# One row of a folded DFT on other engines, earlier folds, and first weight blocks split in idle buffers

## The chip, the cores and the metric

The kernel runs on one core of one Trainium2 chip. Its engines are TensorE (PE in the profile; its weight loads are PEld), VectorE (DVE), ScalarE (ACT), GpSimd (POOL) and SyncE (SP), which issues most of the DMAs. Each engine works through its own queue in order and waits on semaphores for the others. The metric is the time of one execution on the device in microseconds; the median of the runs counts.

## What is computed

Attention masked by clusters of keys and queries, then a block that adds the real part of a two-dimensional Fourier transform, normalizes and runs an MLP, then a second MLP whose gate goes through a convolution over three tokens. Cut to what matters:

```python
def _attn_ref(q, k, v, centroids):            # 2 batches, 8 heads, 768 tokens, 64 wide
    mask = q_assign[:, :, :, None] == k_assign[:, :, None, :]   # nearest of 16 centroids
    scores = np.where(mask, scale * np.matmul(q, k.transpose(0, 1, 3, 2)), -1e9)
    attn = np.exp(scores - np.max(scores, axis=-1, keepdims=True))
    attn = attn / (np.sum(attn, axis=-1, keepdims=True) + 1e-09)
    return np.matmul(attn, v)

def _moe_ref(x, w_ch1, w_ch2):                # 512 -> 2048 -> 512
    u = x + np.real(np.fft.fft(np.fft.fft(x, axis=1), axis=2))
    un = (u - mean(u)) / np.sqrt(var(u) + 1e-06)
    return u + np.maximum(un @ w_ch1, 0.0) @ w_ch2

def _moe2_ref(x, w_in, conv_w, w_out):        # 512 -> 1024 -> 512
    h = np.maximum(x @ w_in, 0.0)
    gate = 1.0 / (1.0 + np.exp(-conv3(h, conv_w)))
    return h * gate @ w_out
```

The weights come as 64-bit words and are turned into float32 on the chip.

## The kernel before

**Precision.** Most products run in three passes (`pass3`, L84): each operand is a high part plus a low part (the value minus its high part), and high x high, high x low and low x high are summed. A "low part" is thus one elementwise subtraction, and a "high part" one cast.

**Attention** is a loop over 96 steps n (L791), six for each of the 16 heads, in an order written out by hand: within it each engine's queue holds the instructions as the code emits them. Step n computes the scores of step n + 8 with their row maxima (`score_max`, the maximum on VectorE, L571), the transposed scores and their exponentials for step n (`score_exp`: t products L601 and L603, exp on ScalarE L609), the high part of step n - 1's probabilities (`prob_hi`, L621, on ScalarE; on VectorE after step 87) and their low part (`prob_lo`, L629: on VectorE for the steps in `LO_ON_DVE`, on GpSimd for the others), and the product with V of step n - 3 (`attn_v`, L641). The scores, the t products and everything that borrows a bank take turns in three PSUM slots, so a t product needs the slot whose maximum was taken shortly before. Other work is hung into the steps with `at(list, step, function)`; within a step the lists come in the order pre, mid (inside `score_max`), aft, post, fill. So for each following pair of heads: loads, `prep_sims`, `prep_first` (L450, GpSimd), `prep_pick` (L454 and L456, VectorE), high and low parts of queries and keys (`prep_hi`, `prep_lo`: L490 to L499), `prep_turn`. At the end of each head `attn_out` divides and writes to U (L649 to L654); head 7, the last one of the first batch, is written at step 52. `max_turn` (L575 to L580) turns each head's maxima into a row that SP copies to where the t products read it.

**Mixing** (`mixing`, L95) is the Fourier transform of one batch by its symmetries. It folds U into even and odd halves (`fold`, L113 to L118), makes the one row that the fold leaves over ("row", L135 to L137), adds the halves ("even", L142), splits them (L122, L126), multiplies by cosines and sines (y, z, ab) and adds the result to U (`ab_add` L227, `ab_mirror` L235, on GpSimd). The first batch's stages hang in steps 54 to 76 (`plan`, L702); both of its folds run on GpSimd. The second batch's run beside the first MLP, as a generator (`later`, L991) that advances one stage or a few at each `next(side)`.

**Norm** (`norm`, L246) takes a batch's tiles of 128 tokens one at a time: statistics (L255 to L259, VectorE), a power on GpSimd (L264), scaling (L269), four transposes (L274), a copy on ScalarE and a low part on VectorE (L286). The first batch's six tiles start at steps 73, 76, 79, 82, 85 and 88.

**First MLP.** Per batch g and block f of 128 hidden columns: `mlp1_up` (24 matmuls, relu on ScalarE L872, low part on VectorE L874), then `down` (18 matmuls into six accumulators; after the tokens' tiles in `when` it advances the side work). The loop (L1019) does the up product of block f + 1 ahead of the down product of block f. In the first batch each weight block is loaded by SP into one of two `raw64` buffers, converted (`from64`: L299, L300, L302 and L304 on VectorE, L301 on ScalarE), squared for its norm (`squares`, L323, ScalarE) and split (`split_w`: wh by ScalarE L851, wl by VectorE L853). Blocks 0 and 1 are converted ahead during attention; block 0 is split into four mixing buffers from step 92 on (`first_split`). Blocks 9 to 15 have buffers only once the second batch's mixing has given back its pool (L997 to L1000). What lies outside the hand-written loop is placed into the queues by a planner of the compiler, which may issue an instruction earlier than the code has it.

**Second MLP**: as the first, with the convolution between. The change does not touch it.

## Time and profile before

| | us |
|---|---|
| runs shown (3) | 700.31, 701.77, 703.11; median 701.77 |
| profiled execution | 702.69 |
| its span, first to last instruction | 700.9 |
| around the span | 1.79 |
| TensorE busy | 667.3 |
| TensorE idle in the span | 33.6 |
| VectorE, ScalarE, GpSimd busy | 543.9, 410.8, 200.3 |
| attention's steps 0 to 95, start of the first t product to start of the last | 26.6 to 275.4 |
| first MLP's first up product starts | 280.3 |

The profile is one execution. An engine's busy time counts its own instructions only. In a timeline each line gives the start, the length, the engine, the line of the code, the operation, what is written and read, the shape and the count; in brackets stands how long the engine was idle before it and what ended that. Matmuls overlap in the array, so their lengths add up to more than the time they take; their starts tell the pace.

### The profile page before, as it was taken

Reading aid. Unit: us, or ns where it says so; the run is one execution under the profiler, and the core shown is the slowest. Engines: PE = TensorE matmul, PEld = TensorE weight load, DVE = VectorE, ACT = ScalarE, POOL = GpSimd, SP = SyncE. Lnnn points to the kernel's source line nnn. Section 1 sums busy time; section 2 is a strip of 40 time slices with the busy share of each in tenths; the row PEclk is TensorE's granted clock in tenths of the full one; section 3 lists DMA queues with packets and bytes.
Section 4 is the critical chain, followed back from the end, with each engine's and each line's share of the span. In section 5 each row is a group of like instructions: output and inputs, shape, how many; then the busy total and the mean of one; then the engine's idle time right before and its main releaser. Section 6 shows DMA issues by size and latency. Waiting matters only on the chain.

```text
span 700.9 us, 12789 instructions
## 1 busy us (share of the span) xinstructions
PE 667.3 (95%) x5106; PEld 504.6 (72%) x5106; DVE 543.9 (78%) x873; ACT 410.8 (59%) x664; POOL 200.3 (29%) x168
## 2 busy tenths in 40 slices
PE   8799999998899997989999999999999999999997
PEld 6598988987799886869998998555555555555553
DVE  7777889898877997999469976997634399867662
ACT  3478869787458787536335654676534367555442
POOL 8156658568646945121041000000000000000000
PEclk9999999999899999999999999999999999999999
DMA  7747696773633413224203350243000000001002
GB/s 219 198 110 193 158 244 157 213 209 84 155 87 78 106 62 122 68 98 144 113 0 121 121 180 10 77 156 122 0 2 1 1 0 1 1 1 71 20 1 90
DMA packets 22087, 66.50 MB, mean 95 GB/s; under 512 B 4502, under 2 KB 7562, under 8 KB 19212
## 3 DMA queue, kind: packets, MB, share of 16 engines
q1 hardware_dynamic: 21020, 61.94, 31.0%
q0 software_dynamic: 1008, 3.75, 2.0%
q8 instruction: 40, 0.66, 0.4%
q14 instruction: 19, 0.16, 0.1%
HBM read 40.94 MB, written 5.77 MB: 67 GB/s over the span
## 4 chain that ended last, share of the span: by engine, by line
PE 72%; DVE 16%; DMA 4%; issue 2%; ACT 2%; POOL 2%; SPq 1%; DVEq 0%; ACTq 0%; POOLq 0%
PE acc L86 8%; PE acc L87 8%; PE acc L85 8%; PE up L85 5%; PE up L87 5%; PE up L86 5%; PE av L641 5%; PE s L566 3%; PE t L601 3%; PE s L568 3%; PE t L603 3%; DVE m L571 3%; PE sim L440 3%; PE u L85 2%; PE u L87 2%
## 5 line engine op out<-in xcount | busy, mean ns | idle before, releaser
L629 POOL TENSOR_TENSOR p<-p,p 128x768 f16<-128x768 f32 x62 | 107.5, 1735 | 85.7 <-ACT p L621 59.5
L571 DVE TENSOR_REDUCE m<-s 128x1 f32<-128x768 f32 x96 | 90.5, 947 | 13.8 <-PE s L568 6.5
L609 ACT ACTIVATE p<-t,cbias 128x768 f32<-128x768 f32 x92 | 82.8, 900 | 26.2 <-PE t L603 25.0
L621 ACT CAST p<-p 128x768 f16<-128x768 f32 x88 | 73.0, 830 | 1.2
L641 PE MATMUL av<-V,p 128*128 128x65 f16 x1728 | 70.8, 195 | 2.8 <-POOL p L629 2.8
L641 PEld LDWEIGHTS <-p 128*128 128x128 f16 x1728 | 59.3, 99 | 18.3 <-issue 15.1
L601 PE MATMUL t<-X 128*128 128x384 f32 x192 | 54.5, 365 | 8.6 <-DVE m L571 6.9
L566 PE MATMUL s<-X 128*128 128x384 f32 x192 | 56.2, 374 | 3.2 <-DMA X<-ohd 1.8
L568 PE MATMUL s<-Y 96*128 96x384 f32 x192 | 50.0, 341 | 1.1 <-DMA Y<-G 1.1
L603 PE MATMUL t<-Y 98*128 98x384 f32 x192 | 50.2, 343 | 0.0
L85 PE MATMUL up<-un,wha 128*128 128x384 f32 x120 | 41.3, 344 | 2.7 <-DVE YcL L163 1.3
L85 PE MATMUL u<-x,wb 128*128 128x384 f16 x128 | 41.7, 326 | 1.3 <-DVE h L892 0.9
L87 PE MATMUL up<-un,wla 128*128 128x384 f32 x120 | 40.5, 338 | 1.8 <-DVE wla L853 1.8
L601 PEld LDWEIGHTS t<-X 128*128 128x128 f32 x192 | 32.0, 192 | 13.9 <-issue 6.7
L85 PE MATMUL up<-un,wa 128*128 128x384 f16 x128 | 41.7, 326 | 0.0
L87 PE MATMUL up<-un,wa 128*128 128x384 f16 x128 | 41.7, 326 | 0.0
L86 PE MATMUL up<-un,wa 128*128 128x384 f16 x128 | 41.7, 326 | 0.0
L87 PE MATMUL u<-x,wb 128*128 128x384 f16 x128 | 41.7, 326 | 0.0
L86 PE MATMUL u<-x,wb 128*128 128x384 f16 x128 | 41.7, 326 | 0.0
L86 PE MATMUL up<-un,wha 128*128 128x384 f32 x120 | 40.5, 338 | 0.0
L629 DVE TENSOR_TENSOR p<-p,p 128x768 f16<-128x768 f32 x30 | 37.7, 1257 | 0.1
L85 PE MATMUL acc<-wb,gH 128*128 128x512 f16 x96 | 36.4, 379 | 0.5 <-ACT gH L900 0.5
(368 smaller groups left out, 1701.0 us busy)
## 6 DMA issues: line engine op xcount, KB each, us to landing
rawa<-w SPq DMA_DIRECT2D x14, 1024.0 KB
rawb<-w SPq DMA_DIRECT2D x8, 1024.0 KB
raw<-qk SPq DMA_DIRECT2D x7, 768.0 KB
X<-G SPq DMA_DIRECT2D x14, 384.0 KB
Y<-G SPq DMA_DIRECT2D x14, 384.0 KB
vraw<-v SPq DMA_DIRECT2D x8, 384.0 KB
out<-y SPq DMA_DIRECT2D x12, 256.0 KB
X<-G SPq DMA_DIRECT2D x14, 192.0 KB
```

Of the source, the lines that this page charges most:

```text
L85: T.matmul(o, sH, mH, start=start, stop=False)
L86: T.matmul(o, sH, mL, start=False, stop=False)
L87: T.matmul(o, sL, mH, start=False, stop=stop)
L566: T.matmul(t[:, c, 0:384], X[:, 0, sl], X[:, 1, 384 * c:384 * c + 384], start=True, stop=False)
L568: T.matmul(t[:, c, 0:384], Y[0:96, 0, sl], Y[0:96, 1, 384 * c:384 * c + 384], start=False, stop=True)
L571: V.tensor_reduce(m6s[h][:, i:i + 1], t[:, :, 0:384], AX.XY, ALU.max, negate=True)
L601: T.matmul(t[:, c, 0:384], X[:, 1, sl], X[:, 0, 384 * c:384 * c + 384], start=True, stop=False)
L603: T.matmul(t[:, c, 0:384], Y[0:98, 1, sl], Y[0:98, 0, 384 * c:384 * c + 384], start=False, stop=True)
L609: A.activation(p, t[:, :, 0:384], AF.Exp, bias=cbias, scale=0.125)
L621: A.copy(p16[:, 0], p32s[n])
L629: eng.tensor_sub(p16[:, 1], p, p16[:, 0])
L641: T.matmul(o, p16[:, k, 128 * j:128 * j + 128], v16[:, i, h % 2, 65 * part:65 * part + 65], start=(i + j + k + part == 0), stop=(i == 5), ...
```

## The change

- The mixing's "row" is cut into four stages: a subtraction on GpSimd (step 54), a copy on ScalarE (56), a subtraction on GpSimd (56), a copy on ScalarE (58). Before, it was three instructions on VectorE at step 57. The second batch's row changes with it.
- The first batch's even folds start at steps 52 and 53 instead of 54 and 55.
- Low parts of steps 55, 71, 79, 83 and 85 go from VectorE to GpSimd, that of step 94 from GpSimd to VectorE. The two low parts of the last pair of heads (`prep_lo`, step 69) go from GpSimd to VectorE.
- Norm's six tiles start at steps 72, 75, 78, 80, 83 and 85.
- The bfloat16 identity is made at step 84 on GpSimd; before, it was made outside the loop on VectorE.
- The first up product of the MLP stands in the attention loop, at steps 96 and 97, in attention's PSUM slots; block 0 is split at steps 91 to 94; block 1 is split into the mixing's buffers YcH and YcL at steps 96 and 97.
- The squares of blocks 0 and 1 move to rounds 11 and 12 of the first MLP. Round f (1 to 13) asks for block f + 2; before, round f (0 to 12) asked for block f + 3. The conversions are issued one block after another. Round 0 advances the side work once, not twice.

```diff
 LO_ON_DVE = ({n for n in range(54) if n % 12 in (2, 7, 8, 10)}
-             | {n for n in range(54, 87) if n % 12 in (1, 2, 7, 11)} | {87})
+             | {59, 61, 62, 67, 73, 74, 86, 87, 94})
...
-            r1 = dp.tile([1, N2], F32, tag="row", bufs=1, name=f"r1{b}")
-            ev = d["ev", 0], d["ev", 1]
-            V.tensor_sub(r1[:, 0:257], ev[0][0:1, 0, 0:257], ev[1][0:1, 0, 0:257])
-            V.tensor_copy(Zx[0:1, 0:257], r1[:, 0:257])
-            V.tensor_sub(Zx[32:33, 0:257], r1[:, 0:257], f32(Zx[0:1, 0:257]))
+            r1 = d["r1"] = dp.tile([1, N2], F32, tag="row", bufs=1, name=f"r1{b}")
+            G.tensor_sub(r1[:, 0:257], d["ev", 0][0:1, 0, 0:257], d["ev", 1][0:1, 0, 0:257])
+
+        @stage("rowH")
+        def _():
+            A.copy(Zx[0:1, 0:257], d["r1"][:, 0:257])
+
+        @stage("rowL")
+        def _():
+            G.tensor_sub(d["r1"][:, 0:257], d["r1"][:, 0:257], f32(Zx[0:1, 0:257]))
+
+        @stage("rowZ")
+        def _():
+            A.copy(Zx[32:33, 0:257], d["r1"][:, 0:257])
...
+    A_LOADS = [()] + [(f + 2,) for f in range(1, 14)] + [()] * 2
...
-        for op in from64(w, raw):
-            op()
+        with tc.issue_after(last_op[0]) if last_op else nullcontext():
+            for op in from64(w, raw):
+                i = op()
+            last_op[:] = [i.ins]
...
-                at(fill, k + 9, prep_lo, m, 0, G)
+                at(fill, k + 9, prep_lo, m, 0, G if m < 7 else V)
...
-                at(fill, k + (10 if m < 7 else 9), prep_lo, m, 1, G)
+                at(fill, k + (10 if m < 7 else 9), prep_lo, m, 1, G if m < 7 else V)
...
-        plan = (("even0", fill, 54), ("even1", fill, 55), ("row", aft, 57), ("even", fill, 58), ("evenH", aft, 59),
-                ("evenL", fill, 59),
+        plan = (("even0", fill, 52), ("even1", fill, 53), ("row", fill, 54), ("rowH", aft, 56), ("rowL", fill, 56),
+                ("even", fill, 58), ("rowZ", fill, 58), ("evenH", aft, 59), ("evenL", fill, 59),
...
-        for i, t in enumerate((0, 3, 1, 4, 2, 5)):
-            n = 73 + 3 * i
+        for n, t in zip((72, 75, 78, 80, 83, 85), (0, 3, 1, 4, 2, 5)):
...
-        at(fill, 92, first_split, 0)
-        at(fill, 93, first_split, 1)
-        at(fill, 95, first_split, 2)
-        at(fill, 97, first_split, 3)
+        def first_up(i):
+            if i == 0:
+                hs[0, 0, 0] = [dp.tile([128, 780], F32R, tag=t, bufs=1, name=f"first{t}")[:, 0:S] for t in ("e0", "e1")]
+            h, tk = hs[0, 0, 0], slice(384 * i, 384 * i + 384)
+            o = slot(f"up0_{i}")[:, 0, 0:384]
+            up_half(o, ws[0, 0, 0], uns[0], i)
+            A.activation(h[0][:, tk], o, AF.Relu)
+            V.scalar_tensor_tensor(h[1][:, tk], o, 0.0, f32(h[0][:, tk]), ALU.max, ALU.subtract)
+
+        def second_split(i):
+            w = [t.rearrange("p a n -> p (a n)") for t in (YcH, YcL)]
+            if i:
+                V.tensor_sub(w[1], w32["a", 1], f32(w[0]))
+                ws[0, 0, 1] = [t[:, 512 * j:512 * j + 512] for j in range(2) for t in w]
+            else:
+                A.copy(w[0], w32["a", 1])
+
+        at(fill, 84, G.tensor_copy, identb, ident)
+        at(post, 96, second_split, 0)
+        at(post, 97, second_split, 1)
+        at(fill, 91, first_split, 0)
+        at(fill, 92, first_split, 1)
+        at(fill, 93, first_split, 2)
+        at(fill, 94, first_split, 3)
+        at(post, 96, first_up, 0)
+        at(post, 97, first_up, 1)
...
-    V.tensor_copy(identb, ident)
...
-                w = ws[0, g, f] = split_w(hp, 3, "a", f, f"a{g}_{f}", V)
+            w = ws[0, g, f] = ws.get((0, g, f)) or split_w(hp, 3, "a", f, f"a{g}_{f}", V)
...
-    mlp1_up(0, 0)
-    for f in range(2):
-        squares("a", f, cvs[0].tile([128, 2048], I32, tag="raw64", bufs=2, name=f"junk{f}")[:, 0:256].bitcast(BF16))
     load_w("a", 2)
...
-            down(0, g, f, side, (1, 4) if g == 0 else (2,))
-            if g == 0 and f + 3 < 16:
-                load_w("a", f + 3)
+            down(0, g, f, side, (1, 4) if g == 0 and f else (2,))
+            for i in A_LOADS[f] if g == 0 else ():
+                load_w("a", i)
+            if g == 0 and f in (11, 12):
+                raw = cvs[0].tile([128, 2048], I32, tag="raw64", bufs=2, name=f"junk{f}")
+                squares("a", f - 11, raw[:, 0:256].bitcast(BF16))
```

## Rows read from the trace of the kernel before

**Rows 1.** The page: its head, part 1, and part 2's granted clock (40 slices, tenths).

```profile
span 700.9 us, 12789 instructions
...
PE 667.3 (95%) x5106; PEld 504.6 (72%) x5106; DVE 543.9 (78%) x873; ACT 410.8 (59%) x664; POOL 200.3 (29%) x168
...
PEclk9999999999899999999999999999999999999999
```

**Rows 2.** Stretches of 10 us: length, busy time (instructions) by engine, granted clock, DMA share, GB/s.

```profile
170.00:180.00 10.00, 4.58 (x44) 3.74 (x43) 8.79 (x10) 3.87 (x8) 10.00 (x6) 0.85 0.07 20
...
180.00:190.00 10.00, 10.00 (x103) 9.37 (x101) 8.66 (x9) 7.06 (x10) 6.62 (x6) 0.81 0.90 213
```

**Rows 3.** Timeline of PE, steps 56 to 59: start, length, line, count, [idle before].

```profile
165.80 0.51 PE L601 MATMUL t<-X 128*128 128x384 f32 x2
...
167.89 0.62 PE L601 MATMUL t<-X 128*128 128x384 f32 x2
...
178.18 0.98 PE L601 MATMUL t<-X 128*128 128x384 f32 x2 [5.34 <-DVE m L571]
```

**Rows 4.** Timeline of DVE: the first batch's row and the maximum behind it; the second batch's row.

```profile
171.37 1.85 DVE L135 TENSOR_TENSOR r<-ev,ev 1x257 f32<-1x257 f32 x1 [1.13 <-POOL ev L115]
...
177.09 0.94 DVE L571 TENSOR_REDUCE m<-s 128x1 f32<-128x768 f32 x1
...
297.13 0.41 DVE L135 TENSOR_TENSOR r<-ev,ev 1x257 f32<-1x257 f32 x1
```

**Rows 5.** Timeline of POOL, steps 51 to 59.

```profile
156.01 3.31 POOL L629 TENSOR_TENSOR p<-p,p 128x768 f16<-128x768 f32 x2 [3.47 <-ACT p L621]
...
161.89 1.66 POOL L629 TENSOR_TENSOR p<-p,p 128x768 f16<-128x768 f32 x1 [2.57 <-issue]
...
164.39 0.20 POOL L113 TENSOR_TENSOR ev<-U 128x3 f32<-128x3 f32 x1
...
169.49 1.85 POOL L115 TENSOR_TENSOR ev<-U 128x765 f32<-128x765 f32 x1
...
178.44 2.49 POOL L629 TENSOR_TENSOR p<-p,p 128x768 f16<-128x768 f32 x1
```

**Rows 6.** Timeline of PE: later pauses, from step 75 to the third MLP block.

```profile
235.46 0.63 PE L274 MATMUL unT<-ident,y 128*128 128x128 f32 x4 [0.65 <-DVE d L651]
...
268.74 0.67 PE L641 MATMUL av<-V,p 128*128 128x65 f16 x16 [1.23 <-POOL p L629]
...
272.68 0.58 PE L601 MATMUL t<-X 128*128 128x384 f32 x2 [1.18 <-DVE d L649]
...
279.22 1.23 PE L641 MATMUL av<-V,p 128*128 128x65 f16 x34 [1.59 <-POOL p L629]
...
285.52 0.44 PE L85 MATMUL up<-un,wha 128*128 128x384 f32 x1 [0.76 <-DVE firste L874]
...
306.91 0.45 PE L87 MATMUL up<-un,wla 128*128 128x384 f32 x1 [1.75 <-DVE wla L853]
...
310.25 0.45 PE L85 MATMUL up<-un,wha 128*128 128x384 f32 x1 [1.31 <-DVE YcL L163]
```

**Rows 7.** Timeline of ACT: a copy of one row; a square of a weight block.

```profile
213.21 0.36 ACT L206 COPY a<-a384p 1x258 f32<-1x258 f32 x1 [0.54 <-PE a384p L199]
...
266.59 0.63 ACT L323 ACTIVATE junk<-wa 128x512 bf16<-128x512 f32 x1
```

**Rows 8.** Groups by line, steps 70 to 90: count, busy us, mean ns, idle before.

```profile
L629 POOL TENSOR_TENSOR p<-p,p 128x768 f16<-128x768 f32 x12 | 20.8, 1740 | 12.6 <-ACT p L621 11.3 <-issue 1.1 <-POOL U L235 0.2
...
L629 DVE TENSOR_TENSOR p<-p,p 128x768 f16<-128x768 f32 x7 | 7.3, 1039 | 0.0
```

**Rows 9.** Timeline of DVE in the first MLP: a weight's conversion; the last weight's low part.

```profile
300.56 2.38 DVE L299 TENSOR_SCALAR wa<-rawa 128x1024 int32<-128x1024 int32 x1
...
417.83 1.23 DVE L853 TENSOR_TENSOR wla<-wa,wha 128x1024 fp32r<-128x1024 f32 x1 [2.96 <-ACT wha L851]
```

**Rows 10.** Timeline of PE: the up product of block 15 starts.

```profile
424.99 0.42 PE L85 MATMUL up<-un,wha 128*128 128x384 f32 x1
```

20 lines of the change are left out of this document (8 added, 12 removed).

## Prediction, before the changed kernel was run

> **What bounds the kernel now.** I read the page first, then the busy times in stretches of 10 us, then TensorE's own timeline for its pauses, then the engine that ended each pause. TensorE is busy for 667.3 of 700.9 us [rows 1], so no change that leaves its work alone can gain more than the 33.6 us of pauses and the time it loses at a low clock. The change leaves its matmuls as they are; it can only close pauses. The reader is to see where they lie. The largest by far is one of 5.34 us before step 59's t product [rows 3]; behind it come a group of four of 0.76 to 1.59 us where attention ends, two of 1.75 and 1.31 us in the first MLP's third and fourth up products, and one of 0.65 us at step 75 [rows 6].
>
> What ended the large pause is VectorE's maximum (L571) at 177.09. VectorE had come to the "row" stage at 171.37, after waiting 1.13 us for GpSimd's second fold, and three instructions on one partition kept it until the small ones before the maximum: 5.5 us in all [rows 4]. The same instruction of the second batch took 0.41 us where the first batch's took 1.85 [rows 4]. Step 59's t product needs the PSUM slot which that maximum empties. [...] Stage price: 5.34 + 2.8 = 8.1 us.
>
> **The change part by part.**
>
> **Folds and row: 5.0 us gained.** VectorE loses the three row instructions and the low part of step 55. Four instructions take their place on GpSimd and ScalarE. ScalarE's two are copies of one row; a like copy took 0.36 us [rows 7], and I take 0.4 each, beside other work (if that cover is gone, 0.8 in all). GpSimd's two subtract 257 elements of one partition. No row shows that; 3 elements took 0.20 and 765 took 1.85 us [rows 5], so each lies between these, by length about 0.75. Does GpSimd become late instead? Before, it stood idle for 3.47 and 2.57 us just ahead of this stage, and from 161.89 to the end of step 58's low part, 178.44 + 2.49 = 180.93, it worked without a break [rows 5]. Out of that run go two folds of 0.20 + 0.20 + 1.85 = 2.25 us, 4.5 together, which now start at steps 52 and 53; in come step 55's low part, 3.31 / 2 = 1.65, and the row's 1.5. Of the folds' 4.5 us the idle 2.57 takes its part and 1.9 spill over. The run then ends at 180.93 - 4.5 + 1.65 + 1.5 + 1.9 = 181.5; about 0.8 of that is the last low part's own delay beside VectorE (2.49 against 1.65), so 180.7 is as likely. TensorE without the pause would be at step 59 at 178.18 - 5.34 = 172.84; steps follow each other in 167.89 - 165.80 = 2.1 us [rows 3], so step 61's attn_v, which reads step 58's low part, comes between 177.0 and 179.1, say 177.8. It waits for some 3.1 us there, in two or three short pieces rather than one. Elsewhere the clock row shows full speed [rows 1] beside pauses of up to 1.8 us [rows 6], so I expect no fall of the clock. Gain 8.1 - 3.1 = 5.0; bounds 3.0 (both row instructions at 1.85 us) and 8.1 (GpSimd not waited for). At step 55 VectorE's prep_pick now waits for GpSimd's product, which stands behind the folds; queued behind that wait is the step's maximum, some 0.7 us late by the same shift, and the low part taken from VectorE right after it gives 1.04 back [rows 8].
>
> [...] In rows: the one-partition row took 1.85 us with GpSimd at work and 0.41 in the second batch [rows 4]. [...]
>
> **Low parts and norm, steps 69 to 88: 0.6 gained.** Steps 71, 79, 83 and 85 go to GpSimd at 1.74 us each, 7.0; two low parts of the last head pair leave it, about 2 x 1.7 = 3.5 as an estimate from the same size; the bfloat16 identity comes, 128 columns, so between 0.20 and 1.85 [rows 5] and near the lower, 0.5. Net 4.0 us against 12.6 us that it waits there [rows 8]: no cost, provided that the waits lie near (if not, up to 4.0). VectorE gets rid of four at 1.04 [rows 8]. Norm's first tile starts a step earlier, so its scaling is no longer behind the mixing's last additions: the pause of 0.65 goes (bounds 0 and 0.65).
>
> **Attention's tail: 3.8 gained.** Four pauses, 1.23 + 1.18 + 1.59 + 0.76 = 4.8 us [rows 6]. The first follows ScalarE: four squares of the MLP's first weights, 0.63 each [rows 7] plus a short read of the sum, stood among its casts; they go to rounds 11 and 12, where TensorE does not wait for them. The second is gone with norm's last tile, which leaves steps 88 to 92. The third waits for GpSimd's low part of step 94, which is now VectorE's (1.04 against 1.74 us [rows 8]), and 24 matmuls of the first up product stand ahead of the last attn_v products to fill it. The fourth, for VectorE's low part of the first relu, shrinks since no conversion of weights need stand ahead of it. New in the tail: a weight copy on ScalarE and a low part on VectorE (1.23 us by its like, rows of L853 [rows 9]); ScalarE has the squares' 2.5 us for it, VectorE the moved tile. On SP's queue the load of block 2 may now stand ahead of the last head's two rows of maxima, which step 90 needs; no row shows that pair waiting, so nothing to 1 us. I leave 1.0 for all that these delay. Bounds: 1.0 and 4.8.
>
> **Start of the first MLP: 1.3 gained.** The pauses of 1.75 and 1.31 us [rows 6] are VectorE's: wla of block 3 and YcL stood behind a conversion whose instruction took 2.38 us beside GpSimd's fold [rows 9]. The conversions now stay in order among themselves, each is asked for a round later, and round 0 takes one side step for two. But GpSimd's folds still run there, with two row instructions more. I take somewhat under half of 3.1; bounds 3.1 and minus 3.
>
> **Late weights: 0.5 lost.** Block 15's low part was done at 417.83 + 1.23 = 419.06 and its up product began at 424.99 [rows 9, 10]: 5.9 us to spare. The pool of blocks 9 to 15 opens half a round later (2 to 4 us), and the two junk tiles take one of two raw buffers for about 2 us each. That is 6 to 8 against 5.9: 0 to 2, I take 0.5; the upper bound is the second rival.
>
> Sum: 5.0 + 0.6 + 3.8 + 1.3 - 0.5 = 10.2 us. The profiled execution took 702.69 us, span and 1.79 us around it, so 692.5; it lies 0.9 above the median of 701.77, against which the forecast is **691.6**.
>
> **The rivals.**
>
> First, VectorE keeps the tail. The third weight's raw tile no longer waits for the squares, so its conversion may be issued between the casts of steps 88 to 97, four instructions of 1.2 to 2.4 us [rows 9]. For it: VectorE ended the pauses of 1.18 and 0.76 [rows 6]. Against: it loses norm's tile there. Tail 1.0 and start 0 instead of 3.8 and 1.3: a gain of 6.1, 695.7.
>
> Second, and slower: the weights come too late. A round asks for block f + 2 and the next round's first matmuls read it. If the conversion ends only with its own round, then the cast (about 1.2, twice a half block's 0.63 [rows 7]) and the low part (1.23 [rows 9]) follow after the up product should have begun: with the hand-overs some 2.6 us in each of blocks 9 to 15, 18 us, and 701.8 - 10.2 + 18 = 709.6. It decides from the point at which the conversions run more than 5.9 us later than now [rows 9, 10]. Against it: VectorE waited 2.96 us before that low part [rows 9], so it has room and runs ahead of its round.
>
> Third, the lock. Five low parts more on GpSimd at 1.65 to 1.74 us may hold VectorE 8 us in steps 55 to 86, and TensorE would come 8 us later to the tail: gain 2, 699.6. Against it: VectorE's own low parts there took 1.04 us in the mean beside a GpSimd that was busy for most of the time [rows 8]. [...]
>
> Fourth, the change does not free the row: the first fold needs head 7's output, written at step 52 itself, and GpSimd then stands waiting with low parts queued behind it. Fold stage 0 instead of 5.0: 696.6. Against it: GpSimd is idle for 3.47 us right before [rows 5].
>
> **How the numbers follow.** Forecast 0.62, VectorE's tail 0.17, slower weights 0.08, the lock 0.07, no freed row 0.06. A measurement of this kernel can tell about 0.5% (3.5 us) from no change: below 698.3 is faster, above 705.3 slower. Faster: 0.60 of the forecast, 0.14, 0.03 and 0.02 of the first, fourth and third rival, 0.79. Same: 0.13. Slower: the second rival, 0.08. The range reaches down to all pauses gone, 8.1 + 0.65 + 4.8 + 3.1 = 16.6, rounded to 685.3 after 0.1 of the late weights, and up to the lock's 699.6; the second rival and little else is left out.
>
> **What would show it.** Right: no pause over 2 us before steps 59 to 61, clock at full level from 170 to 190, GpSimd unbroken until about 180; the pauses that remain before steps 60 and 61 ended by GpSimd's L629; the first up product's matmuls ahead of the last attn_v; wla of block 15 ready before its up product. Wrong: VectorE's conversion instructions between steps 88 and 97; pauses ended by wla in blocks 9 to 15; step 62 less than 3 us earlier than now; VectorE's low parts well over 1.04 us.

## The result: 712.1 us, where 691.6 was forecast

The changed kernel takes 712.11 us (median of 4 runs, 709.05 to 713.15) against 701.82 us before: a ratio of 1.014, 95% interval 1.0101 to 1.0179. It is slower, by about as much as I expected it to gain. The profiled execution took 713.15 us, of which the span is 711.4.

The page of the changed kernel (head, part 1, granted clock in tenths over 40 slices); it answers to [rows 1]:

```profile
span 711.4 us, 12797 instructions
...
PE 673.6 (95%) x5106; PEld 509.9 (72%) x5106; DVE 549.8 (77%) x864; ACT 413.7 (58%) x668; POOL 209.8 (29%) x175
...
PEclk9999999998899999989999999999999999999999
```

TensorE has the same 5106 matmuls and is busy 6.3 us longer: the same work at a lower clock (mean granted clock 0.982 of full speed against 0.994). Its idle time rose from 33.6 to 711.4 - 673.6 = 37.8 us. To find where, I cut the span at instructions which both kernels have: the first t product of a step, and the first matmul into the accumulators (acc) of a block of the first MLP. All stages below are differences of such starts, the last one up to the end of SyncE's last DMA issue.

| stage, us | before | after | difference | forecast |
|---|---|---|---|---|
| up to step 52 | 154.6 | 156.0 | +1.4 | 0 |
| step 52 to 62 (folds, row) | 34.1 | 39.8 | +5.7 | -5.0 |
| step 62 to 75 | 42.4 | 42.5 | 0 | 0 |
| step 75 to 88 (norm, low parts) | 30.8 | 35.7 | +4.9 | -0.6 |
| step 88 to block 0's acc (tail) | 27.8 | 23.8 | -4.1 | -3.8 |
| block 0 to 12 of the first MLP | 122.6 | 125.2 | +2.6 | -1.3 |
| block 12 to the end | 285.4 | 285.8 | +0.4 | +0.5 |

The code up to step 52 is the same in both kernels, and that stage lay between 152.4 and 156.4 us in all runs; its 1.4 is no effect of the change.

**The folds.** Stretches of 10 us of the changed kernel (columns as in [rows 2]); the last is the first MLP's:

```profile
170.00:180.00 10.00, 2.76 (x23) 2.46 (x24) 8.21 (x5) 2.35 (x4) 5.89 (x5) 0.67 0.01 2
180.00:190.00 10.00, 9.04 (x87) 7.82 (x86) 6.39 (x7) 8.02 (x13) 6.46 (x5) 0.82 0.33 76
...
310.00:320.00 10.00, 6.75 (x21) 5.50 (x20) 8.95 (x8) 4.80 (x9) 5.61 (x3) 0.67 0.29 105
```

The granted clock, which was to stay full, stood at 0.50 of full speed for 6.6 + 3.6 = 10.2 us in the first two (173.5 to 183.7), against 6.8 us before (177.0 to 183.8; [rows 2]). It fell in one long pause. (Two shorter ones, 1.14 and 1.44 us, follow in the stage; TensorE's idle time there rose by 4.8 us, from 5.4 to 10.2, which is most of the stage's 5.7.) TensorE, VectorE and GpSimd of the changed kernel around the long pause (timelines; compare [rows 3 to 5]):

```profile
177.24 1.01 PE L614 MATMUL t<-X 128*128 128x384 f32 x2 [7.30 <-DVE m L584]
```

```profile
168.00 0.55 DVE L467 TENSOR_REDUCE m<-eq 128x24 f16<-128x384 f16 x1 [0.40 <-POOL eq L463]
168.59 7.72 DVE L469 TENSOR_TENSOR oh<-desc,m 128x384 f16<-128x384 f16 x1
176.24 0.94 DVE L584 TENSOR_REDUCE m<-s 128x1 f32<-128x768 f32 x1
```

```profile
167.93 0.73 POOL L134 TENSOR_TENSOR r<-ev,ev 1x257 f32<-1x257 f32 x1
168.62 3.24 POOL L642 TENSOR_TENSOR p<-p,p 128x768 f16<-128x768 f32 x2
171.83 0.72 POOL L142 TENSOR_TENSOR r<-r,Zx 1x257 f32<-1x257 f32 x1
172.51 1.62 POOL L642 TENSOR_TENSOR p<-p,p 128x768 f16<-128x768 f32 x1
174.10 1.79 POOL L512 TENSOR_TENSOR G<-raw,G 128x768 fp32r<-128x768 f32 x1
182.66 1.64 POOL L642 TENSOR_TENSOR p<-p,p 128x768 f16<-128x768 f32 x1 [6.76 <-ACT p L634]
```

The row is off VectorE, as planned, and cost GpSimd what I said (0.73 and 0.72). But VectorE's comparison in `prep_pick`, 0.56 us where nothing is in its way (0.80 at this step before), took 7.72. It began while the row's first instruction ran, and ended 0.42 us after the last of GpSimd's unbroken run had ended (174.10 + 1.79 = 175.89). GpSimd gave VectorE no turn between any two of these instructions. The next maximum stood behind the comparison, and step 57's t product waited 7.30 us for that.

**Norm's steps and the first MLP.** Later pauses of TensorE in the changed kernel, against [rows 6]; then VectorE ahead of the second of them:

```profile
240.14 0.63 PE L283 MATMUL unT<-ident,y 128*128 128x128 f32 x4 [0.46 <-ACT p L622]
...
271.16 0.62 PE L579 MATMUL s<-X 128*128 128x384 f32 x2 [1.93 <-DVE m L584]
...
293.41 0.45 PE L85 MATMUL up<-un,YcH 128*128 128x384 f32 x1 [0.60 <-DVE firste L778]
...
313.70 0.69 PE L85 MATMUL up<-un,wha 128*128 128x384 f32 x1 [2.62 <-ACT wha L883]
```

```profile
266.80 2.43 DVE L561 SCALAR_TENSOR_TENSOR V<-vraw,vsc,V 128x768 f16<-128x768 f32 x1
269.16 0.68 DVE L264 BATCH_NORM_STATS2 st<-U 128x6 f32<-128x512 f32 x1
...
270.16 0.95 DVE L584 TENSOR_REDUCE m<-s 128x1 f32<-128x768 f32 x1
```

The values' scaling took 2.43 us here beside GpSimd and 1.00 with norm where it was, in e5_norm_back below; with a tile's statistics between it and the maximum, TensorE waited 1.93. Three more pauses of 0.67 to 0.77 us stand between steps 75 and 88; all of TensorE's idle time there is 4.9 us instead of 1.5. The pauses of 1.23, 1.18 and 1.59 us at the attention's end [rows 6] are gone or 0.2 us. In the MLP pauses of 2.62 and 0.63 took the place of 1.75 and 1.31. From block 0 to block 12 TensorE's idle time is nearly the same, 4.3 us against 4.0, and its work is the same, 622 matmuls; what is new is that the granted clock fell at the pause of 2.62, to 0.50 of full speed for 6.8 us (313.4 to 320.2), where before it stayed at 1.00. In this profile, then, nearly all of the stage's 2.6 us is the clock.

### The profile page after: what moved, and what is told of

Read it like the earlier page. It is cut to its first block, busy times and chain, and to the rows that moved or that the text cites. A ratio compares the mean times of both kernels' runs of the same rounds, so it can differ in the third digit from the quotient of the medians.

```text
span 711.4 us, 12797 instructions
## 1 busy us (share of the span) xinstructions
PE 673.6 (95%) x5106; PEld 509.9 (72%) x5106; DVE 549.8 (77%) x864; ACT 413.7 (58%) x668; POOL 209.8 (29%) x175
## 3 DMA queue, kind: packets, MB, share of 16 engines
q1 hardware_dynamic: 21020, 61.94, 30.4%
## 4 chain that ended last, share of the span: by engine, by line
PE 61%; DVE 25%; DMA 5%; ACT 4%; issue 2%; POOL 1%; SPq 1%; DVEq 0%; ACTq 0%; POOLq 0%
PE acc L87 6%; PE acc L86 6%; PE acc L85 6%; PE up L85 4%; PE up L87 4%; PE up L86 4%; DVE m L584 4%; PE av L654 4%; PE s L579 3%; PE t L614 3%; PE s L581 3%; PE t L616 2%; PE sim L453 2%; PE u L85 2%; PE u L87 2%
## 5 line engine op out<-in xcount | busy, mean ns | idle before, releaser
L642 POOL TENSOR_TENSOR p<-p,p 128x768 f16<-128x768 f32 x66 | 113.1, 1716 | 92.9 <-ACT p L634 66.6
L654 PE MATMUL av<-V,p 128*128 128x65 f16 x1728 | 72.4, 197 | 0.2 <-POOL p L642 0.2
L85 PE MATMUL up<-un,wha 128*128 128x384 f32 x112 | 39.4, 352 | 3.4 <-ACT wha L883 3.4
L87 PE MATMUL up<-un,wla 128*128 128x384 f32 x112 | 38.3, 347 | 0.9 <-DVE wla L885 0.9
L86 PE MATMUL up<-un,wha 128*128 128x384 f32 x112 | 38.7, 346 | 0.0
L579 PEld LDWEIGHTS s<-X 128*128 128x128 f32 x192 | 30.1, 193 | 11.6 <-DVE m L584 6.4
L85 PE MATMUL acc<-wb,gH 128*128 128x512 f16 x96 | 36.4, 379 | 0.5 <-ACT gH L928 0.5
```

Source lines behind the costliest of these rows:

```text
L85: T.matmul(o, sH, mH, start=start, stop=False)
L86: T.matmul(o, sH, mL, start=False, stop=False)
L87: T.matmul(o, sL, mH, start=False, stop=stop)
L579: T.matmul(t[:, c, 0:384], X[:, 0, sl], X[:, 1, 384 * c:384 * c + 384], start=True, stop=False)
L642: eng.tensor_sub(p16[:, 1], p, p16[:, 0])
L654: T.matmul(o, p16[:, k, 128 * j:128 * j + 128], v16[:, i, h % 2, 65 * part:65 * part + 65], start=(i + j + k + part == 0), stop=(i == 5), ...
```

## Experiments

Each is timed against the kernel before on the same chip, except the four profiles named at their place. The stages of all of them (us, from one profiled run each; the last stage is the first MLP from block 0 to block 12, which four of the expectations below call blocks 0 to 6):

| kernel | 52 to 62 | 75 to 88 | tail | MLP 0 to 12 | median | ratio (95%) |
|---|---|---|---|---|---|---|
| before_again | 34.2 | 30.8 | 27.9 | 122.6 | - | - |
| after_again | 39.8 | 36.3 | 23.1 | 126.3 | - | - |
| e1_fold_back | 33.2 | 36.2 | 23.3 | 126.4 | 705.61 | 1.0051 (1.0031 to 1.0071) |
| e2_pick_psum | 35.5 | 36.2 | 22.6 | 127.2 | 705.82 | 1.006 (1.0028 to 1.0092) |
| e3_lo_back | 34.6 | 35.4 | 23.6 | 125.0 | 709.78 | 1.0106 (1.0072 to 1.0139) |
| e4_row1_dve | 39.6 | 34.9 | 23.0 | 124.4 | 710.22 | 1.0112 (1.0059 to 1.0165) |
| e5_norm_back | 39.4 | 30.4 | 25.7 | 125.4 | 707.90 | 1.0075 (1.0044 to 1.0106) |
| e6_wide_row | 31.5 | 36.4 | 23.0 | 126.3 | 705.23 | 1.0053 (1.0032 to 1.0075) |
| e7_loads_back | 40.0 | 34.9 | 23.0 | 125.4 | 710.44 | 1.0127 (1.0101 to 1.0153) |
| c1_wide_norm | 33.6 | 30.4 | 25.7 | 126.0 | 702.97 | 1.0001 (0.998 to 1.0022) |
| c2_less_dve | 33.9 | 30.4 | 25.7 | 124.5 | 701.20 | 0.9986 (0.9961 to 1.0011) |
| c3_tail_only | 33.9 | 30.4 | 25.7 | 125.2 | 701.88 | 0.9994 (0.9973 to 1.0016) |
| c4_fold_wide | 33.6 | 30.9 | 27.9 | 124.5 | 701.47 | 0.9984 (0.9959 to 1.0009) |
| c5_fold_wide_psum | 34.2 | 30.9 | 27.9 | 122.6 | 702.01 | 1.0006 (0.9988 to 1.0024) |
| c6_all_mended | 35.5 | 30.3 | 24.9 | 125.2 | 700.66 | 0.9978 (0.9956 to 0.9999) |
| c7_no_psum | 33.6 | 30.3 | 25.7 | 124.7 | 699.94 | 0.9965 (0.9938 to 0.9992) |

The two unchanged kernels profiled again show the stages to repeat within 0.1 us before, and within 1.2 after. Where kernels share a stage's code, though, it can differ by more: the folds of the changed kernel took 39.4 to 40.0 us in five profiles and 34.6 in e3_lo_back's, the mended folds 33.6 to 33.9 in four (c1, c2, c4, c7) and 31.5 in e6_wide_row's. The profiled run is the lowest of its kernel's runs in e3_lo_back, the second lowest in e5_norm_back and e6_wide_row, and the highest in c4_fold_wide and c6_all_mended. A stage's difference of 1 or 2 us between two kernels is therefore weak evidence by itself.

### Which part costs: folds and row, low parts, or the second row

```diff
# e1_fold_back: b == 0 has the three VectorE instructions of before again, at step 57
+             | {55, 59, 61, 62, 67, 73, 74, 86, 87, 94})
...
+        plan = (("even0", fill, 54), ("even1", fill, 55), ("row", aft, 57), ("rowH", aft, 57), ("rowL", aft, 57),
# e3_lo_back
+             | {59, 61, 62, 67, 71, 73, 74, 79, 83, 85, 86, 87, 94})
# e4_row1_dve: for b == 1 the three VectorE instructions of before, the other stages empty
+            if b in (1,):
...
```

> The changed kernel with its fold stage put back for the first batch alone: folds at steps 54 and 55, row on VectorE at step 57, low part of step 55 on VectorE. [...] Rival (the loss is in steps 75 to 88 and in the MLP, the fold stage only shifts it): 710 to 713.

> The changed kernel with the low parts of steps 71, 79, 83 and 85 back on VectorE. [...] Rival (norm's tiles, two or three steps apart instead of three, crowd VectorE and the PSUM slots): nothing gained or 1 to 2 us lost, 711 to 714.

> The changed kernel with the second batch's row alone back on VectorE. Theory A (its two copies wait on ScalarE for GpSimd, 2.94 and 1.19 us, with the weight copy wha of block 3 queued behind them, and so make the pause of 2.6 us before that block's up product and the low clock after it): 3 to 5 us gained, 707 to 709. Rival (VectorE's conversions, now in order, and GpSimd's fold are what is late): 0 to 1 us gained.

With the folds and the row back the time falls to 705.61 us, 6.5 below the changed kernel, and the old pause of 5.3 us before step 59 returns: this part costs what the stage says. The low parts are not it: steps 75 to 88 stayed at 35.4. e3_lo_back's fold stage, whose code is the changed kernel's, was shorter in its profiled run because the comparison took 3.70 us instead of 7.72; that run, at 704.79, is the lowest of its seven. VectorE and GpSimd there:

```profile
165.83 3.70 DVE L469 TENSOR_TENSOR oh<-desc,m 128x384 f16<-128x384 f16 x1
```

```profile
165.87 3.24 POOL L642 TENSOR_TENSOR p<-p,p 128x768 f16<-128x768 f32 x2
169.08 1.03 POOL L142 TENSOR_TENSOR r<-r,Zx 1x257 f32<-1x257 f32 x1
170.07 1.64 POOL L642 TENSOR_TENSOR p<-p,p 128x768 f16<-128x768 f32 x1
171.69 1.81 POOL L512 TENSOR_TENSOR G<-raw,G 128x768 fp32r<-128x768 f32 x1
```

Here VectorE got its turn after two of GpSimd's instructions, with three still to come; in the five other profiles of this code it waited for all (7.72 or 7.73 us). Why it got one here is not known. The second batch's row explains at most 0.8 to 1.9 us of the MLP (124.4 against 125.2 and 126.3 in the changed kernel's two profiles).

### What makes VectorE wait so long

Two edits leave every instruction in its place. One takes an SBUF input from the comparison (its maxima go to one of the three PSUM slots, as float32 instead of float16), the other gives both of GpSimd's row instructions 128 partitions.

```diff
# e2_pick_psum
-            m2 = ep.tile([128, 24], F16, tag="m2", bufs=1, name=f"m2{m}")
+            m2 = slot(f"m2{m}")[:, 0, 0:24] if m == 6 else ep.tile([128, 24], F16, ...)
# e6_wide_row
-            G.tensor_sub(r1[:, 0:257], d["ev", 0][0:1, 0, 0:257], d["ev", 1][0:1, 0, 0:257])
+            G.tensor_sub(r1[:, 0:257], d["ev", 0][:, 0, 0:257], d["ev", 1][:, 0, 0:257])   # r1: 128 partitions
```

> The changed kernel with one tile moved: the 24 maxima that prep_pick of head pair 6 compares at step 55 are written to a PSUM slot, so that its comparison has one SBUF input and one PSUM input. [...] Rival C (GpSimd's run itself is the next limit): the pause shrinks to 3 us before steps 59 to 61, 3 to 5 us gained, 707 to 709.

> The changed kernel with the row's two subtractions on GpSimd done on all 128 partitions instead of on one (127 of them are worked out for nothing); every instruction stays in its place and about as long, 0.7 us. In the changed kernel a VectorE comparison with two SBUF inputs took 7.72 us and ended only when GpSimd's unbroken run of instructions, which began with such a subtraction on one partition, had emptied. [...] Rival (any unbroken run of GpSimd locks VectorE out until its queue has a gap): the stretch stays at 36 to 40 us, the time at 709 to 713.

VectorE in e2_pick_psum; then VectorE and GpSimd in e6_wide_row (timelines):

```profile
167.04 0.56 DVE L469 TENSOR_TENSOR oh<-desc,m 128x384 f16<-128x384 f16 x1
...
173.65 6.55 DVE L151 TENSOR_TENSOR ev<-ev,ev 128x771 f32<-128x771 f32 x1
```

```profile
166.05 2.10 DVE L469 TENSOR_TENSOR oh<-desc,m 128x384 f16<-128x384 f16 x1
```

```profile
165.39 0.74 POOL L134 TENSOR_TENSOR r<-ev,ev 128x257 f32<-128x257 f32 x1
166.09 3.56 POOL L642 TENSOR_TENSOR p<-p,p 128x768 f16<-128x768 f32 x2
```

With one input in PSUM the comparison took its 0.56 us beside the same GpSimd run, with both in SBUF 7.72: that input makes the difference, and not its type, since m1_lock below shows the wait for float16 and float32 alike (10.73 and 11.33 us). The wait went to the next instruction with two SBUF inputs, the even sum (6.55 us; 0.94 where nothing is in its way), so that 6.3 us were won. With the row on 128 partitions the comparison took 2.10 us, a wait for one GpSimd instruction, and GpSimd's second then waited for the comparison: two take 3.56 us instead of 3.24. The stage fell from 39.8 to 31.5 us (33.6 to 33.9 in the four other profiles of these folds), and the time to 705.2. So for the comparison it is the one-partition instruction, not its length (0.73 us on one partition, 0.74 on 128) or place.

A kernel of its own measures this alone: after a small subtraction of 257 columns, GpSimd does six more of 128x768 without a pause, and VectorE's instruction is released by the small one.

```diff
+        G.tensor_sub(first[0:rows, 0:257], a[0:rows, 0:257], b2[0:rows, 0:257])   # rows 128, 1, 16, 32, 64
+        for k in range(6):
+            G.tensor_sub(qs[k], a, b2)
+        V.tensor_sub(dv, first, b2)
```

> A kernel of its own that leaves out the whole computation and measures one thing: how long VectorE's instruction takes beside an unbroken run of GpSimd. In each of 20 phases GpSimd does a subtraction on 128x768, then a small one of 257 columns on 128, 1, 16, 32 or 64 partitions, then six more subtractions on 128x768; VectorE's instruction (a subtraction of float32 128x768, or a comparison of float16 128x384, both with two SBUF inputs) is released by the small one. [...] Rival (any run locks it out): it takes the whole run in all phases. Second rival (never more than one instruction): 1 to 3 us in all phases, and the long waits of the changed kernel have another cause.

VectorE's instruction after 128, 1 and 64 partitions, and the small instruction itself by its form (count | busy, mean ns):

```profile
5.88 2.54 DVE L72 TENSOR_TENSOR dv<-first,b 128x768 f32<-128x768 f32 x1 [0.58 <-POOL first L68]
...
59.50 11.33 DVE L72 TENSOR_TENSOR dv<-first,b 128x768 f32<-128x768 f32 x1 [11.15 <-POOL first L68]
...
224.00 11.33 DVE L72 TENSOR_TENSOR dv<-first,b 128x768 f32<-128x768 f32 x1 [2.66 <-POOL first L68]
```

```profile
L68 POOL TENSOR_TENSOR first<-a,b 128x257 f32<-128x257 f32 x4 | 2.9, 724 | 0.0
L68 POOL TENSOR_TENSOR first<-a,b 64x257 f32<-64x257 f32 x4 | 2.9, 719 | 0.0
```

After 128 partitions the wait is one instruction of GpSimd (all four times: 2.54 us in all with float32, 1.94 with float16); after 1, 16, 32 or 64 it is the whole run (all sixteen times: 11.33 and 10.73). The small instruction takes the same 0.72 us each time.

After 128 partitions there was such a wait too: c5_fold_wide_psum (in the last part) had one, 6.90 us for the even sum, with no instruction on fewer partitions in sight. I looked for its cause in a second kernel of this kind, with twice 20 phases: later requests, full instructions between, 3 columns, long runs, float16 output, an instruction with a PSUM input beside it.

> A kernel of its own that leaves out the whole computation, as m1_lock: what makes VectorE's instruction with two SBUF inputs (a subtraction, float32 128x768, 0.8 to 1 us alone) wait out more than one of GpSimd's. Open is why c5_fold_wide_psum still had a wait of 5.96 us over the rest of GpSimd's run, with the row on all 128 partitions. Twice 20 phases; in each GpSimd has an instruction that waits for VectorE, then some others, then six full subtractions without a pause. Varied: by how much VectorE's request comes after the start of the six (0 to 3 copies with one input ahead of it); a small instruction on 128 partitions or on 1 directly ahead, or on 1 and then full ones; instructions of 3 columns; long runs of full ones; float16 output; an instruction of VectorE with one input in PSUM beside the run. Theory S2 (only instructions on fewer partitions do it, and their effect stays until GpSimd's queue has a gap): all phases with an instruction on one partition last to the end of the six, whatever the delay, all others wait one instruction at most, some 1 to 2.5 us. Rival S3 (the length of GpSimd's run without a meeting, or VectorE's instruction with an input in PSUM, does it as well): the phases with six full ones ahead, with two rows of 257 columns or with the PSUM input wait for several too.

VectorE in m2_lock: one partition directly ahead; one partition and then three full instructions:

```profile
62.59 10.57 DVE L83 COPY cpy<-first 128x64 f32<-128x64 f32 x1 [4.11 <-POOL first L69]
73.08 0.94 DVE L86 TENSOR_TENSOR dv<-first,b 128x768 f32<-128x768 f32 x1
...
143.88 1.77 DVE L83 COPY cpy<-first 128x64 f32<-128x64 f32 x1 [8.11 <-POOL first L67]
145.58 2.60 DVE L86 TENSOR_TENSOR dv<-first,b 128x768 f32<-128x768 f32 x1
```

In the phases without a one-partition instruction VectorE's instructions waited, as I read that trace, for one of GpSimd's at most; no line of them stands here. (After the fourth of them, with three more copies, VectorE stood idle for 4.11 us until the first line above; after a wait to the end it was 2.66.) This speaks against run length, columns, type and the PSUM input as causes, and against rival S3. S2 holds in part: with the one-partition instruction directly ahead, or one full one between, the wait lasted to the end of the run (10.57 us both times); with three full ones between, it was one instruction again (1.77 and 2.60). A copy with a single input is caught too (10.57 us for 64 columns). The even sum's wait of 6.90 us in c5_fold_wide_psum is not explained by this and stays open. Nor can e2_pick_psum's 6.55 us be put down to the one-partition row: the same instruction waited at the same place in c5_fold_wide_psum and c6_all_mended, where the row has 128 partitions. These are the three kernels with the comparison's maxima in PSUM; in the others the even sum took 0.94 to 1.66 us.

### Norm's places

```diff
+        for n, t in zip((73, 76, 79, 82, 85, 88), (0, 3, 1, 4, 2, 5)):
```

> The changed kernel with one part undone: the six tiles of norm stand at steps 73, 76, 79, 82, 85 and 88 again instead of 72, 75, 78, 80, 83 and 85. The low parts stay as the change has them. In the changed kernel the stretch from the transform of step 75 to that of step 88 took 35.7 us instead of 30.8, and e3_lo_back showed that the low parts do not carry this. Theory (the tiles stand too close together for VectorE, whose sums for norm come late, and TensorE pauses): the stretch falls to 31 to 32.5 us, of the tail's 4 us some 0 to 2 are lost again since norm ends later, and the kernel takes 708 to 710 us, 2 to 5 less than the changed one. Rival (the stretch is long by what the folds left behind, a shifted order of GpSimd and VectorE, not by norm's places): it stays at 35 to 36 us and the time at 711 to 713.

As the theory has it, steps 75 to 88 went back to 30.4 us, and the tail kept 2.1 of its 4.1. Both stages together: 58.7 before, 59.5 changed, 56.1 so. The closer places moved 1.9 us from the tail into the stage (four transposes, 0.6 us, and pauses) and added 3.4 of pauses and clock.

### The first MLP

```diff
# e7_loads_back
+    A_LOADS = [(f + 3,) for f in range(13)] + [()] * 3      # no issue_after; side steps (1, 4) in round 0
# c2_less_dve, on c1_wide_norm: the last VectorE instruction of the conversion left out for blocks 2, 3, 4
+            for op in from64(w, raw)[:4 if k == "a" and 2 <= f < 5 else 5]:
```

> The changed kernel with the first MLP's supply put back: its weights' loads are issued one block earlier per step as before, the conversions no longer wait for the last one of the block before, and the side steps of the first batch stand as before. The first blocks stay split in the mixing's buffers and the first product stays in the attention's loop. In the changed kernel the stretch from the first output sum of block 0 to that of block 12 took 125.2 us instead of 122.6, with a pause of TensorE of 2.62 us for a converted weight. Theory (the new order of supply makes that pause): the stretch falls to 122.5 to 123.5 us and the kernel takes 709 to 710.5 us. Rival (the second batch's row on GpSimd and ScalarE, or the split blocks, make it): it stays at 125, the time at 711 to 713.

> As c1_wide_norm, with one instruction of VectorE's conversion left out for the weight blocks 2, 3 and 4 (the last of the five, which puts zeros in place of the smallest values; 1.22 us each by the row L314), so three instructions or 3.7 us of VectorE less while the first MLP starts. Theory (VectorE sets the pace of the MLP's first blocks, where it was busy 42.1 of 45.8 us in the changed kernel and 42.8 of 44.7 before; that is why the earlier start was given back): the stretch from the first output sum of block 0 to that of block 6 falls by 3 to 4 us, from 125.4 to 121.5 to 122.5. Rival (the supply is set by the order of loads or by ScalarE's queue): it falls by under 1 us.

The order of supply is not the cause of the stage's length: 125.4. The pauses add up to 5.7 us there, and the clock did not fall; 1.1 us of its 2.8 over the kernel before are neither and are not explained. Taking 3.7 us from VectorE won 1.4 against c1_wide_norm, under half of what the theory asks. One pause of 4.52 us took the place of 2.68 and 1.71, and all pauses of the stage add up to 5.3 us against 5.5; what differs is the clock, at 0.50 of full speed for 3.4 us instead of 6.8. The stretches of blocks 0 and 1 and of blocks 2 and 3, before and then in the changed kernel (VectorE is the third pair), and that pause in c2_less_dve:

```profile
289.84:312.48 22.64, 19.32 (x96) 16.82 (x96) 21.98 (x25) 10.40 (x22) 7.01 (x6) 1.00 0.28 94
312.48:334.55 22.07, 22.07 (x114) 20.16 (x114) 21.49 (x24) 13.72 (x26) 1.97 (x1) 1.00 0.50 175
```

```profile
297.75:315.15 17.40, 14.50 (x65) 12.20 (x65) 16.16 (x19) 9.78 (x19) 8.74 (x6) 0.95 0.27 97
315.15:343.50 28.35, 27.72 (x135) 25.59 (x135) 26.47 (x26) 14.69 (x30) 5.49 (x4) 0.91 0.36 127
```

```profile
308.44 0.44 PE L85 MATMUL y<-DC,EH 128*128 128x386 f32 x1 [4.52 <-DVE hL L902]
```

VectorE was busy 43.5 of 44.7 us before and 42.6 of 45.8 in the changed kernel, and what ended the pause was a low part of VectorE that stood behind conversions. So VectorE ends this pause, but that its load sets the stage's length is not shown: with less of it the pauses stayed, though the median fell (701.20 against 702.97).

Then the two unchanged kernels once more, one profile each:

> The kernel before, unchanged, profiled once more: how much of the stages' differences is the clock's luck. c4_fold_wide, whose MLP is that of before, had the stretch from the first output sum of block 0 to that of block 6 at 124.5 us instead of 122.6, with pauses of TensorE as in before but the clock at half for 6.8 us behind them. Theory (the fall of the clock behind these pauses is not the change's): this run too shows a half clock near the first output sums and 124 to 125 us in this stretch. Rival (the kernel before keeps its clock there and the change loses it): 122.5 to 123 us and no half clock from 280 to 330 us. The fold's stretch from step 52 to step 62 should be 33 to 34.5 us in both cases, with one pause of about 5.3.

> The changed kernel, unchanged, profiled once more. Theory (the wait of VectorE behind the row on one partition comes in every run, its length by where GpSimd's queue empties): the stretch from step 52 to step 62 is 38 to 40 us with a pause of 7 us or so, that from step 75 to step 88 35 to 36, the MLP's blocks 0 to 6 take 124.5 to 126. Rival (the profiled run was an extreme one): the fold's stretch is below 37 us.

The kernel before showed 122.6 us and a full clock again, so luck does not explain all. The changed kernel's stages came again too, with the comparison at 7.73 us and the MLP at 126.3 (pauses of 5.4 us instead of 4.3). But luck explains some: c4_fold_wide and c5_fold_wide_psum have the MLP of before, 124.5 and 122.6 us. Stretches of both, c4_fold_wide first (columns as above, the clock third from the end):

```profile
300.00:310.00 10.00, 7.31 (x33) 5.76 (x32) 10.00 (x10) 2.02 (x3) 4.30 (x3) 0.89 0.00 2
310.00:320.00 10.00, 10.00 (x40) 9.31 (x41) 8.15 (x10) 5.56 (x13) 0.00 (x0) 0.77 0.34 110
```

```profile
300.00:310.00 10.00, 6.75 (x33) 5.41 (x32) 10.00 (x10) 2.17 (x5) 4.14 (x3) 1.00 0.01 2
310.00:320.00 10.00, 10.00 (x52) 9.06 (x53) 9.78 (x11) 6.32 (x14) 0.00 (x0) 1.00 0.51 170
```

The pauses ahead are alike, 0.25 and 1.75 us in one and 0.23 and 1.71 in the other; in one run the clock fell to 0.50 of full speed for 6.8 us, in the other it stayed at 1.00. In the changed kernel, where the pause is 2.6 to 3.0 in one piece, the clock fell in every profile but e7_loads_back's, which has shorter ones and more of them.

### The parts put together

c1_wide_norm is e6_wide_row and e5_norm_back in one; c3_tail_only is e1_fold_back and e5_norm_back in one; c4_fold_wide is the kernel before with the early folds, the first batch's row on 128 partitions of GpSimd and step 55's low part there; c5_fold_wide_psum adds e2_pick_psum's edit to it. c6_all_mended is c1_wide_norm with that edit and the second row on VectorE, and c7_no_psum is that without the edit.

> The changed kernel with two parts mended together: the row's subtractions on GpSimd on all 128 partitions (as in e6_wide_row) and norm's tiles back at steps 73 to 88 (as in e5_norm_back). Theory (the folds, norm's steps and the tail with the first MLP add up as measured one by one): against the kernel before, the stretch from the transform of step 52 to that of step 62 is 2.6 us shorter, that from step 75 to the first output sum 2.6 shorter, and the first MLP's blocks 0 to 6 give 2.8 back; the sum is -2.4 and the time 699 to 700.5 us. Rival (a stall that one part lifts comes back beside the other): 702 to 705.

> The changed kernel with the first batch's folds, its row and the low part of step 55 as before (as in e1_fold_back) and norm's tiles as before (as in e5_norm_back): what is left of the change is the other low parts, the attention's tail, the first MLP's start and the second batch's row. Theory (the tail's gain is given back in the first MLP, since VectorE is the bound there): the stretch from the transform of step 75 to the first output sum is 2 to 3 us shorter than before, that of the MLP's blocks 0 to 6 as much longer, and the time is within 1.5 us of the kernel before, 701 to 703. Rival (the tail's gain stays, as the sum of the prediction has it): 697 to 699.

> The kernel before with one part of the change alone, mended: the first batch's even folds start at step 52, its row stands at steps 54 to 58 on GpSimd and ScalarE with GpSimd's subtractions on all 128 partitions, and the low part of step 55 is GpSimd's. The second batch's row, norm, tail and MLP are those of before. Theory (the prediction's first term holds once GpSimd's instructions have all partitions): the stretch from the transform of step 52 to that of step 62 falls from 34.1 to 31 to 32 us, the clock's fall behind it is gone or shorter, and the kernel takes 698 to 700 us. Rival (the fold's pause is replaced by others, by the low part given to GpSimd or by waits one instruction long): the stretch stays at 33.5 to 35 us and the time at 701 to 703.

> c4_fold_wide with one thing more: the maxima that pair 6's comparison reads are written to PSUM, so that this comparison has one input in SBUF (as in e2_pick_psum). In c4_fold_wide the comparison took 2.11 us, beside GpSimd's instruction of 3.58 for two, where it takes 0.56 alone, and TensorE paused 1.69 us behind it. Theory (what is left of the fold's time are VectorE's instructions with two SBUF inputs that each wait out one of GpSimd's): the pause of 1.69 goes, the clock's fall behind it too, the stretch from step 52 to step 62 falls from 33.6 to 30.5 to 32 us and the kernel takes 698.5 to 700.5 us. Rival (the next such instruction waits in its place): 33 to 34 us, and 701 to 702.5.

> The changed kernel with all that the runs pointed to: the row's subtractions on GpSimd on 128 partitions, norm's tiles at steps 73 to 88, the comparison of pair 6 with its maxima in PSUM, and the second batch's row on VectorE, so that its even sum need not wait for GpSimd's row. Theory (the mended folds gain 2 to 3 us and the tail 2, the MLP gives 0 to 1 back against a run of before with its clock's fall): 698 to 700 us. Rival (GpSimd's added work costs VectorE one instruction at each meeting, so that the sum stays where it was): 701 to 703.

> c6_all_mended without the maxima in PSUM: the changed kernel with the row of the first batch on 128 partitions, that of the second on VectorE, and norm's tiles at steps 73 to 88. c6_all_mended's profile showed the comparison free but the even sum waiting 5.95 us in its place. Theory (the comparison's wait of one instruction lines the two engines up, so that the sum behind it waits for one only): the stretch from step 52 to step 62 is 33.6 us as in c1_wide_norm instead of 35.5, and the kernel takes 699 to 701 us, faster than before by 0.1 to 0.4%. Rival (the second batch's row on VectorE brings nothing, and c1_wide_norm's time comes again): 702 to 704.

Alone and mended, each part is worth nothing that can be measured; c1_wide_norm, c4_fold_wide and c5_fold_wide_psum came out as their rivals, c3_tail_only as its theory, and c6_all_mended (700.66) between its two. The tail gains 2.1 us and the MLP gives 2.6 back (c3_tail_only). The mended folds gain 0.6 (c4_fold_wide), since TensorE's one pause of 5.3 us became several of the same sum: 0.40, 1.69, 1.79 and 1.43, each ended by VectorE behind an instruction that waited out one of GpSimd's. Only the clock's fall is shorter (3.4 us), and in e6_wide_row, with pauses of 4.9 us in sum, it did not fall at all: that is most of the stage's 31.5 against 33.6. The PSUM edit freed the comparison and lost the even sum (c5_fold_wide_psum; VectorE, then GpSimd's run beside it):

```profile
172.97 6.90 DVE L164 TENSOR_TENSOR ev<-ev,ev 128x771 f32<-128x771 f32 x1
```

```profile
172.26 1.83 POOL L521 TENSOR_TENSOR G<-raw,G 128x768 fp32r<-128x768 f32 x1
174.06 1.64 POOL L651 TENSOR_TENSOR p<-p,p 128x768 f16<-128x768 f32 x1
175.66 1.79 POOL L519 TENSOR_TENSOR G<-raw,G 128x768 fp32r<-128x768 f32 x1
177.42 1.62 POOL L651 TENSOR_TENSOR p<-p,p 128x768 f16<-128x768 f32 x1
```

c6_all_mended still had that wait in its profile. All parts together, without the edit, give c7_no_psum, as its theory has it: 699.94 us, ratio 0.9965, 0.35% faster than before and 12 us below the change as it was. It has the row's two stages on 128 partitions, norm at its old steps and the second row on VectorE; all else is the change's. The interval lies clear of 1, but the gain is less than the 0.5% that I had named as the least that can be told.

## Why the prediction was wrong

**What bounds the kernel.** That only pauses and the clock could move held. That the change could only close pauses did not: I counted the pauses it would fill, and no term of the sum held one that it would open.

**Folds and row, -5.0 forecast, +5.7 measured: the step that failed.** GpSimd's and ScalarE's prices were right (0.73 and 0.72 against 0.75; 0.41 against 0.4). What failed is what the working left out: I asked whether GpSimd becomes late, and not what its run does to VectorE's instructions beside it. The stage price of 8.1 holds 2.8 us for the low clock that no row shows as a loss; the profile of the kernel before has the clock at 0.50 of full speed from 177.0 to 183.8 us, 1.2 us of it pause and 5.6 work, where a pair of matmuls of a t product took 0.84 to 0.98 us instead of 0.51 to 0.62, so 2.8 is an estimate from that. The bounds, 3.0 to 8.1, came from GpSimd's own times and held no loss (and the lower one is 2.8 by its own terms: two instructions at 1.85 instead of 0.75). The third rival had VectorE held up by GpSimd, but put it on the low parts, one instruction at a time, 8 us in all, with a chance of 0.07. What I held against it was misread. VectorE's seven low parts with the mean of 1.04 us [rows 8] ran for the most part while GpSimd did nothing: five of them, of 0.94 or 0.95 us, met no instruction of GpSimd at all, and of the two that did one took 1.59 while the other took 0.94 and GpSimd's addition beside it 1.76 where a like one took 1.08. Two of the seven in the kernel before, the first beside GpSimd and the second with GpSimd idle:

```profile
230.01 1.59 DVE L629 TENSOR_TENSOR p<-p,p 128x768 f16<-128x768 f32 x1
...
246.20 0.95 DVE L629 TENSOR_TENSOR p<-p,p 128x768 f16<-128x768 f32 x1
```

So the mean was no evidence that VectorE runs free beside GpSimd. The runs showed it on the row, over a whole run of GpSimd, 7.16 us in one place, and the clock at 0.50 of full speed for 10.2 us around it. That an instruction on one partition holds VectorE off for the whole run could not be read from the rows; that the two engines hold each other up could (1.85 us beside GpSimd and 0.41 later for the row on VectorE [rows 4], 2.49 us and 1.66 for a low part on GpSimd [rows 5]). Even mended, the term was 0.3 to 0.6 us in four profiles and 2.6 in one, not 5.0: the remaining waits are not for step 58's low part, as I worked out, but for VectorE's maxima. Of the signs I named, the one that step 62 comes less than 3 us earlier showed.

**Low parts, -0.6 with norm, +4.9 measured.** That the low parts cost nothing there was right (e3_lo_back). Norm's places I costed as a relief, the pause of 0.65 us at step 75; it fell to 0.46, and what the closer spacing does to VectorE's queue ahead of the maxima was not priced (3.4 us of pauses and clock, by e5_norm_back). The identity took 0.29 us (0.5 taken).

**Tail, -3.8 forecast, -4.1 measured.** The stage is right by luck in part: 1.9 of it only moved ahead with norm's places, into the stage before, and with norm in its old places it is 2.1.

**Start of the MLP, -1.3 forecast, +2.6 measured.** My lower bound was minus 3, so the size lay within; the sign was wrong. I took the order of the conversions to be the cause of the pauses, to be shortened by half; the pauses stayed (4.3 us in sum against 4.0), and e7_loads_back shows that order to change nothing in the stage's length. A fall of the clock was no part of the term, and in the first profile it makes nearly all of the loss. What sets the pauses is not settled: with 3.7 us less of VectorE's work they stayed (c2_less_dve).

**Late weights, 0.5 lost.** The direction was right: block 15's low part ended 2.8 us ahead of its up product (432.67 against 435.45) instead of 5.9 [rows 9, 10]. What the second rival feared, a cast that comes after the up product should have begun, showed in block 9 alone, as a pause of 0.77 us. The rival's 18 us, the only case on the slow side, did not come.

## What to carry to other kernels

Work moved to GpSimd is not priced by its own length: price what VectorE does beside it, one instruction of GpSimd for each VectorE instruction that meets one (a copy of one row took 1.78 us beside GpSimd and 0.28 in the second batch of the kernel before, and the comparison with two SBUF inputs 2.10 instead of 0.56 in e6_wide_row; with an input in PSUM it took 0.56), and look whether GpSimd's queue has gaps. Before a mean is taken as proof that two engines don't disturb each other, look whether they ran at the same time. Keep GpSimd's small leftovers on all 128 partitions (they took the same 0.72 us here, and VectorE's instruction behind them 2.54 us instead of 11.33, m1_lock). And a pause that one engine ends may only break into smaller ones of the same sum if that engine is busy throughout (5.3 us became 0.40, 1.69, 1.79 and 1.43 in c4_fold_wide); ask for its busy share in the stage before counting the pause as a gain.

## What the runs showed of the hardware

- After a GpSimd instruction on 1, 16, 32 or 64 partitions, VectorE got no turn until GpSimd's unbroken run had ended (10.73 and 11.33 us in m1_lock, 16 of 16; behind one on 1 partition 7.72 or 7.73 in five of six profiles of the changed kernel's folds, 3.70 in the sixth), where after one on 128 partitions it waited for one instruction (2.54 and 1.94 us, 4 of 4). Three full instructions without a request between them ended the effect (1.77 and 2.60 us); one did not (10.57 us; m2_lock).
- It caught a VectorE copy with one input as well (10.57 us, 128x64, m2_lock), but not the comparison with its second input in PSUM (0.56 us, e2_pick_psum).
- Why the even sum took 6.90 us instead of 0.94 in c5_fold_wide_psum, and waited 5.95 us in c6_all_mended, with only full-width instructions around it was not found.
- Behind pauses of 0.25 and 1.75 us the granted clock fell in one run (to 0.50 of full speed for 6.8 us in c4_fold_wide, the stage 1.9 us longer), and behind 0.23 and 1.71 in the same code of c5_fold_wide_psum it stayed at 1.00.
